# A MoE stage whose steps are ordered by a planner: talking-heads attention into a SoLU MoE on one core

## The chip, the core and the metric

One Trainium2 chip, one of its cores. The metric is the device time of one execution in microseconds. The core has five engines, each with its own queue that it works through strictly in order: PE (TensorE, matmuls), DVE (VectorE), ACT (ScalarE), POOL (GpSimd) and SP (SyncE, which issues DMAs). An instruction that waits holds everything behind it in its queue.

## The reference, cut to what matters

```python
# attention: batch 4, 12 heads, 448 tokens, head dimension 64
scores = einsum('bhij,hg->bgij', q @ k.T / 8, w_pre);  attn = softmax(scores)
x = (einsum('bhij,hg->bgij', attn, w_post) @ v)  ->  1792 tokens x 768
# MoE: d_model 768, d_ff 1024
h = x @ w_in;  solu = h * softmax(h)
ln = (solu - mean) / sqrt(var + 1e-6) * g_ln
out = ln @ w_out
```

[...] Each fp32 matmul of the MoE is three fp16 matmuls on operands split in a high and a low half (high by high, high by low, low by high).

## The kernel before, in words

**Attention** takes the first two thirds of the run. Its instructions are given as tasks to the class `Plan`: each task names its engine and a duration, the tasks it comes after, a due time, and the ring of buffers that it takes a slot of, with the tasks that free the slot. `Plan.order` simulates the engines: again and again it takes the engine and the task that can start earliest; among the tasks of an engine that can start within 0.143 us of the first one it prefers the one with the smallest due time. What comes out is one list, written into the queues in that order. The planner fixes only the order; semaphores still make each instruction wait for its data.

**The MoE** comes behind that list and is written out by hand. Its unit is a tile of 128 tokens, 14 of them; the three tiles of the last batch, whose x is still on the chip, come first, the other 11 are fetched back from DRAM (`x_fetch`, 6 pieces per batch). For tile t:
- `hidden(t)` (L876): 36 matmuls on PE into one of three PSUM bank pairs. Tile 0's are already in the attention's plan.
- `solu_head(t)`: DVE takes the maximum (L1387), ACT the exponential (L1390).
- `solu_mean(t)`: DVE guards and inverts the sum and multiplies (L1401); that product is the last reader of the bank pair. ACT squares (L1405), DVE forms the variance (L1408), POOL its power -1/2 (L1411).
- `ln(t)`: a Newton step on DVE (L1418 to L1426), POOL applies the norm (L1427), ACT makes the high half (L1430), POOL the low half (L1432).
- `turn(t)`: two transposing DMAs on SP (L1442), into a ring of 9.
- `project(t)`: 48 matmuls (L1458) by w_out into two banks, one for each half of the output columns, then a copy on ACT (L1466) and the store.

**w_out** is converted beside it, in 8 chunks of 128 rows. A chunk is fetched into one of two buffers (`cv`, L775), and goes through `convert_steps`: exponent (DVE, L790), rebias (ACT, L793), sign (DVE, L796), mantissa (DVE, L801), join (DVE, L806), product (POOL, L809); an absmax on ACT (L1351) ends it and frees the buffer. When all 8 are through, the joint maximum is taken on DVE, spread over the partitions by one matmul in PE's queue (L243), and turned into a scale; then each chunk is split into its two halves (high on ACT, L271; low on DVE, L276).

What sets the order is one loop over t. Iteration t issues the second half of tile t's softmax, `project(t - 11)`, `hidden(t + 1)`, the head of tile t + 1, `ln(t)`, the fetch of chunk t + 2 and `turn(t - 1)`. The steps of a chunk stand at lettered places inside (`work(t, "a")` to `"i"`), one chunk for each iteration: exponent and rebias of chunk t + 1 at place d of iteration t, the rest at a to e of the next. The 8 splits stand at places 9h to 10f, and `project(0)` in iteration 11.

Of the kernel before, what the change touches and what calls it, by code (L numbers as in the profile page):

```python
# [152 lines left out]
def kernel(  # L153
# [600 lines left out]

    def x_fetch(b, i, pool):
# [517 lines left out]
    with tc.manual_schedule():  # L1273
# [34 lines left out]
        nc.vector.tensor_tensor(out=ic, in0=i_post, in1=i_wi, op=ALU.mult)  # L1308
        nc.vector.tensor_scalar(out=ib, in0=i_v, scalar1=ic, scalar2=2.0**E_X, op0=ALU.mult, op1=ALU.mult)
        for b in range(B):  # L1310
            t0, t1 = -(-b * S // 128), (b + 1) * S // 128
            nc.vector.tensor_copy(out=ch[:, 0, t0:t1], in_=ib[:, b : b + 1].to_broadcast([128, t1 - t0]))
            n0 = (b + 1) * S - t1 * 128
            if n0:
                nc.vector.tensor_copy(out=ch[0:n0, 0, t1 : t1 + 1], in_=ib[0:n0, b : b + 1])
                nc.vector.tensor_copy(out=ch[n0:128, 0, t1 : t1 + 1], in_=ib[n0:128, b + 1 : b + 2])
        for i, m in ((1, -1.0), (3, 2.0**E_LN)):
            nc.vector.tensor_scalar(out=ch[:, i], in0=ch[:, 0], scalar1=m, scalar2=None, op0=ALU.mult)
        nc.vector.scalar_tensor_tensor(
            out=ch[:, 2], in0=ch[:, 0], scalar=1.0 / DFF, in1=ch[:, 0], op0=ALU.mult, op1=ALU.mult  # L1320
        )

# [20 lines left out]
        def convert_w_out(kc):  # L1343
            if kc % 4 == 0:
                wo_raw.append(raw_p.tile([128, KFF // 2, DM], F32, tag="raw", name=f"wo{kc}"))
            t = wo_raw[kc // 4][:, kc % 4]
            ex = parts64(f"wo{kc}")[2].bitcast(F32)
            exponent, rebias, sign, mantissa, join, product = convert_steps(t, f"wo{kc}")

            def absmax():  # L1350
                nc.scalar.activation(out=ex, in_=t, func=AF.Abs, accum_out=am_o[:, kc : kc + 1])  # L1351

            for i, place, f in zip(
                (kc - 1, kc - 1, kc, kc, kc, kc, kc),
                "ddabcce",
                (exponent, rebias, sign, mantissa, join, product, absmax),
            ):
                fill.setdefault((i, place), []).append(f)
# [14 lines left out]
        def split_w_out(kc):  # L1373
            x = wo_raw[kc // 4][:, kc % 4]
            split_hi(wo_h[:, kc], x, gs_wo[:, kc : kc + 1])
            split_lo(wo_l[:, kc], x, gs_wo[:, kc : kc + 1], wo_h[:, kc])

        lnp = {}

        heads, late = {}, []  # L1380

        def solu_head(t):

            ps = hps.pop(t).rearrange("p n f -> p (n f)")
# [8 lines left out]
        def solu_mean(t):
            ps, sm, u = heads.pop(t)
            v, y = (ms_p.tile([128, 1], F32, tag=n, name=f"{n}_{t}") for n in ("v", "y"))
            nc.vector.tensor_scalar(out=sm, in0=sm, scalar1=1e-9, scalar2=None, op0=ALU.add)
            work(t, "a")
            nc.vector.reciprocal(out=sm, in_=sm)
            work(t, "b")
            su, nmu, sq = (ms_p.tile([128, 1], F32, tag=n, name=f"{n}_{t}") for n in ("su", "nmu", "sq"))  # L1400
            nc.vector.scalar_tensor_tensor(  # L1401
                out=u, in0=ps, scalar=sm, in1=u, op0=ALU.mult, op1=ALU.mult, accum_out=su
            )
            nc.vector.tensor_scalar(out=nmu, in0=su, scalar1=-1.0 / DFF, scalar2=None, op0=ALU.mult)
            nc.scalar.activation(out=junk, in_=u, func=AF.Square, bias=nmu, accum_out=sq)  # L1405
            work(t, "c")
            work(t, "d")
            nc.vector.tensor_scalar(  # L1408
                out=v, in0=sq, scalar1=ch[:, 2, TURNS[t] : TURNS[t] + 1], scalar2=1e-6, op0=ALU.mult, op1=ALU.add
            )  # L1410
            nc.gpsimd.tensor_tensor(out=y, in0=v, in1=half_p, op=ALU.pow)  # L1411
            late.append((u, nmu, v, y))

        def ln(t):

            u, nmu, v, y = late.pop()
            z, rs, nm = (ms_p.tile([128, 1], F32, tag=n, name=f"{n}_{t}") for n in ("z", "rs", "nm"))
            nc.vector.scalar_tensor_tensor(out=z, in0=y, scalar=v, in1=y, op0=ALU.mult, op1=ALU.mult)  # L1418
            work(t, "e")
            nc.vector.tensor_scalar(out=z, in0=z, scalar1=-0.5, scalar2=1.5, op0=ALU.mult, op1=ALU.add)  # L1420
            work(t, "f")
            nc.vector.scalar_tensor_tensor(
                out=rs, in0=z, scalar=ch[:, 3, TURNS[t] : TURNS[t] + 1], in1=y, op0=ALU.mult, op1=ALU.mult
            )
            work(t, "g")
            nc.vector.tensor_scalar(out=nm, in0=nmu, scalar1=rs, scalar2=None, op0=ALU.mult)  # L1426
            nc.gpsimd.tensor_scalar(out=u, in0=u, scalar1=rs, scalar2=nm, op0=ALU.mult, op1=ALU.add)  # L1427
            lh = h_p.tile([128, DFF], F16, tag="lh", name=f"lh_{t}")
            ll = h_p.tile([128, DFF], F16, tag="ll", name=f"ll_{t}")
            nc.scalar.copy(out=lh, in_=u)  # L1430
            work(t, "h")
# [4 lines left out]
        lts = {}

        def turn(t):
            lt = lts[t] = []
            for x, z in zip(lnp.pop(t), "hl"):  # L1440
                y = lt_p.tile([128, KFF, 128], F16, tag=f"t{z}", name=f"lt{z}_{t}")
                nc.sync.dma_start_transpose(out=y, in_=x)  # L1442
                lt.append(y)

        def project(t):
            lt = lts.pop(t)
            o = h_p.tile([128, DM], F32, tag="o", name=f"o_{t}")
            ends = [0, DM // 2, DM] if t < NT - 1 else [0, 2 * DM // 3, DM]
            ys = []
            for n, (c0, c1) in enumerate(zip(ends, ends[1:])):  # L1450
                y = (ps_x, ps_y)[n % 2].tile([128, 512], F32, tag="x", name=f"y{n}_{t}")
                ys.append((y[:, 0 : c1 - c0], slice(c0, c1)))

            for group in [ys] if t == 0 else [[y] for y in ys]:
                for kc in range(KFF):
                    for a, (xx, ww) in enumerate(((lt[0], wo_h), (lt[0], wo_l), (lt[1], wo_h))):
                        for y, cut in group:
                            nc.tensor.matmul(  # L1458
                                y,
                                xx[:, kc],  # L1460
                                ww[:, kc, cut],
                                start=(kc == 0 and a == 0),
                                stop=(kc == KFF - 1 and a == 2),
                            )
# [84 lines left out]
```

## Time and profile before

| | |
|---|---|
| median of 3 runs | 720.27 us (719.42 to 721.44) |
| the profiled execution, its own time | 722.47 us |
| its span, first to last instruction | 720.8 us |
| PE busy | 651.8 us, 90% |
| DVE, ACT, POOL busy | 500.4 (69%), 455.2 (63%), 282.7 us (39%) |
| chain that ended last, by engine | PE 49%, DVE 26%, DMA 8%, ACT 6% |
| mean granted TensorE clock | 0.971 |

A row of instructions gives the line of the kernel, engine, operation, output and input tiles with their shape, and the count. "Idle before" is the time in which the engine stood still just ahead of it, with what released it. PE's durations overlap, since matmuls are pipelined: starts are to be compared with starts. The granted clock is 1.00 at 2.4 GHz and 0.50 at 1.2 GHz; what lies between is a mean over both.

### The profile page before, as it was taken

The page shows a single profiled execution, that of the slowest core. Times are in us where ns is not written, and L with a number is a line of the kernel's source. Part 1 is how long each engine was busy: PE and PEld are TensorE (multiplying, and loading weights), DVE is VectorE, ACT ScalarE, POOL GpSimd, SP SyncE. Part 2 cuts the span into 40 slices and gives each one's busy share as a digit, 9 for nine tenths or more (in the row PEclk, how much of TensorE's full clock was granted, in tenths as well). Part 3 has the DMA queues.
Part 4 walks back from the last instruction along what each step waited for, and adds up shares of the span by engine and source line. Part 5 has one row for each costly group of instructions (what it writes and reads, how often), then busy time and mean ns, then how long its engine had stood idle before and what let it go on. Part 6 is the DMA issues. An engine that isn't in the chain of part 4 may idle for free.

```text
span 720.8 us, 17481 instructions
## 1 busy us (share of the span) xinstructions
PE 651.8 (90%) x6514; PEld 430.3 (60%) x6514; DVE 500.4 (69%) x1331; ACT 455.2 (63%) x977; POOL 282.7 (39%) x447
## 2 busy tenths in 40 slices
PE   1787999999899999799899899899978959999997
PEld 1545767777567777677676677664433424566664
DVE  6977998789977799977899898646888654200000
ACT  1757887998779888788799887414455553321111
POOL 3704682247742257731244235305655523310000
PEclk9899999999999999999999999999999978999999
DMA  9137458456776566997339432057657402263112
GB/s 230 40 78 203 162 148 198 150 184 201 209 152 139 142 200 186 219 208 228 134 134 272 177 93 67 1 166 207 146 125 130 82 1 52 51 117 81 45 51 60
DMA packets 114028, 98.51 MB, mean 137 GB/s; under 512 B 69604, under 2 KB 104600, under 8 KB 113944
## 3 DMA queue, kind: packets, MB, share of 16 engines
q1 hardware_dynamic: 108120, 83.62, 44.0%
q0 software_dynamic: 4416, 12.40, 6.2%
q10 hardware_dynamic: 1408, 1.38, 0.7%
q8 instruction: 51, 0.84, 0.5%
q14 instruction: 33, 0.27, 0.1%
HBM read 33.24 MB, written 9.63 MB: 59 GB/s over the span
## 4 chain that ended last, share of the span: by engine, by line
PE 49%; DVE 26%; DMA 8%; ACT 6%; issue 5%; POOL 4%; SPq 2%; POOLq 0%; DVEq 0%; ACTq 0%
PE y L1458 15%; PE po L659 14%; PE px L708 6%; PE pm L604 5%; PE ps L534 5%; DVE dead L614 5%; DVE s L551 4%; DMA cv_wo<-in_moe_w_out_dram 4%; PE ps_h L876 3%; DMA sr<-s 2%; ACT e L630 2%; DVE hl_k L276 2%; DVE sm L641 2%; DVE hl_q L276 1%; DVE u L1387 1%
## 5 line engine op out<-in xcount | busy, mean ns | idle before, releaser
L659 PE MATMUL po<-wr,e 128*112 128x120 f32 x1440 | 184.6, 279 | 15.3 <-POOL wr L651 12.3
L659 PEld LDWEIGHTS po<-wr,e 128*112 128x112 f32 x1440 | 161.4, 181 | 54.4 <-POOL wr L651 28.4
L651 POOL TENSOR_SCALAR wr<-wq,sm 128x120 f32<-128x120 f32 x180 | 70.8, 403 | 217.4 <-DVE sm L645 124.7
L630 ACT ACTIVATE e<-pm,nb,c_exp 128x448 f32<-128x448 f32 x180 | 131.9, 734 | 23.7 <-DVE dead L614 21.2
L614 DVE TENSOR_SCALAR_CACHE_REDUCE dead<-pm,c_nexp 128x448 f16<-128x448 f32 x180 | 121.6, 675 | 14.6 <-PE pm L604 8.4
L280 ACT COPY p_t<-po 112x480 f32<-112x480 f32 x180 | 109.7, 620 | 28.7 <-PE po L659 27.2
L551 DVE SCALAR_TENSOR_TENSOR s<-ps,s 120x448 f16<-120x448 f32 (+1 forms) x192 | 112.4, 616 | 19.0 <-ACT s L546 17.5
L546 ACT ACTIVATE s<-ps 120x448 f16<-120x448 f32 (+1 forms) x192 | 93.9, 546 | 23.7 <-PE ps L534 20.4
L876 PE MATMUL ps_h<-wi,xf 128*128 128x512 f16 x396 | 91.2, 392 | 6.5 <-DVE u L1401 6.5
L708 PE MATMUL px<-p_t,raw_v 112*64 112x120 f32 (+3 forms) x1632 | 88.2, 259 | 1.9 <-ACT e L630 0.8
L708 PEld LDWEIGHTS px<-p_t,raw_v 112*64 112x64 f32 x1632 | 76.0, 137 | 15.5 <-issue 9.3
L534 PE MATMUL ps<-k,q 64*64 64x448 f16 (+2 forms) x1008 | 79.5, 356 | 5.1 <-DVE s L551 3.3
L1458 PE MATMUL y<-wo_h,lth 128*128 128x384 f16 (+2 forms) x224 | 73.4, 334 | 7.2 <-ACT wo_h L271 7.2
L1458 PE MATMUL y<-wo_l,lth 128*128 128x384 f16 (+2 forms) x224 | 73.4, 334 | 2.2 <-DVE wo_l L276 2.0
L876 PEld LDWEIGHTS <-xf 128*128 128x128 f16 x396 | 40.0, 101 | 56.9 <-issue 13.8
L1458 PE MATMUL y<-wo_h,ltl 128*128 128x384 f16 (+2 forms) x224 | 73.2, 333 | 0.0
L1458 PEld LDWEIGHTS <-lth 128*128 128x128 f16 x448 | 44.6, 99 | 41.6 <-issue 13.5
L604 PE MATMUL pm<-sr,wp_hi 64*64 64x448 f16 x720 | 58.3, 362 | 5.6 <-DMA sr<-s 3.5
L1466 ACT ACTIVATE o<-y,c_out 128x384 f32<-128x384 f32 (+2 forms) x28 | 16.1, 578 | 70.7 <-PE y L1458 70.7
L534 PEld LDWEIGHTS <-q 64*64 64x64 f16 (+2 forms) x1008 | 31.9, 106 | 31.6 <-issue 15.3
L1432 POOL TENSOR_TENSOR ll<-u,lh 128x1024 f16<-128x1024 f32 x14 | 30.4, 2171 | 19.2 <-ACT lh L1430 19.2
L630 ACT ACTIVATION_READ_ACCUMULATOR e<-pm,nb,c_exp 128x1 f32 x180 | 37.7, 209 | 0.0
(180 smaller groups left out, 816.0 us busy)
## 6 DMA issues: line engine op xcount, KB each, us to landing
sr<-s SPq DMA_DIRECT2D x176, 210.0 KB
cv_wi<-in_moe_w_in_dram SPq DMA_DIRECT2D x24, 256.0 KB
cv_wo<-in_moe_w_out_dram SPq DMA_DIRECT2D x8, 768.0 KB
raw_k<-in_k_dram POOLq DMA_DIRECT2D x18, 224.0 KB, 4.0
raw_q<-in_q_dram POOLq DMA_DIRECT2D x18, 224.0 KB, 6.5
raw_v<-in_v_dram POOLq DMA_DIRECT2D x18, 224.0 KB, 5.4
xh<-xsh SPq DMA_DIRECT2D x9, 224.0 KB
xl<-xsl SPq DMA_DIRECT2D x9, 224.0 KB
```

The lines of the kernel that those rows point to most:

```text
L280: nc.scalar.copy(out=out, in_=in_)
L534: nc.tensor.matmul(sps[b, c, h + e][lo:hi], q2[b, g][rows, 2 * j + x, i0 + lo : i0 + hi], k1[b, g][rows, 2 * j + y], start=(a == 0), stop= ...
L546: nc.scalar.activation(out=s_t[b, c][0 : y.shape[0], h, 0], in_=y, func=AF.Copy, scale=2.0**-E_S)
L551: nc.vector.scalar_tensor_tensor(out=t[:, h, 1], in0=y, scalar=2.0**-E_S, in1=t[:, h, 0], op0=ALU.mult, op1=ALU.subtract)
L604: nc.tensor.matmul(pmx[b, u + i][64 * e : 64 * e + 64, 0:S], w[rows], sr[b, u][rows, e, z], start=(a == 0), stop=(a == 2),)
L614: nc.vector.tensor_scalar(out=dead, in0=pmx[b, u][:, 0:S], scalar1=c_nexp[0:UK, b : b + 1], scalar2=None, op0=ALU.mult, op1=ALU.min, accum ...
L630: nc.scalar.activation(out=ee[b, u], in_=pmx.pop((b, u))[:, 0:S], func=AF.Exp, bias=nbs.pop((b, u)), scale=c_exp[0:UK, b : b + 1], accum_o ...
L651: ENG[eng].tensor_scalar(out=w, in0=wq[0:UK, 0 : H * UN], scalar1=sm, scalar2=1.0, op0=ALU.mult, op1=ALU.mult)
L659: nc.tensor.matmul(ps[:, c * 120 : (c + 1) * 120], e[:, c * CP : (c + 1) * CP], w, start=True, stop=True)
L708: nc.tensor.matmul(xps[b, blk, g][e * 64 : e * 64 + 64, i, cut], raws["v", b, p][:, e, c * D : (c + 1) * D], next(x for y, x in block_view ...
L876: nc.tensor.matmul(ps[:, n], xx[:, kc, o : o + 128], ww[:, kc, n * 512 : (n + 1) * 512], start=(kc == 0 and a == 0), stop=(kc == KDM - 1 a ...
L1458: nc.tensor.matmul(y, xx[:, kc], ww[:, kc, cut], start=(kc == 0 and a == 0), stop=(kc == KFF - 1 and a == 2),)
```

## The change

The MoE's loop, its lettered places and the list of places for the splits go. Each step becomes a task of a second `Plan`, with an engine, a duration, a due time and its ring; the plan's order is written behind the attention's. The functions issue the same instructions as before, cut into single steps. The factors (`factors`, the small DVE operations ahead of the MoE), the load of g_ln and the fetches of x are tasks as well. `project` of tile 0 is cut into 16 tasks, one for each chunk of w_out and half of the output.

The due times: tile t at 7.75 t, chunk kc at 9.0 kc (its fetch 12 ahead, its absmax 8 behind), the joint maximum at 70, its spread at 70.5, the scale at 72, the splits at 73 + kc and 74 + kc, output tile t at 7.75 (t + 11).

```diff
-        SPL = "9h 9i 10a 10b 10c 10d 10e 10f".split()
...
-        for t in range(NT + LAG):
-            if t + 1 < KFF:
-                convert_w_out(t + 1)
-            if t < NT:
-                solu_mean(t)
-            if 0 <= t - LAG < NT:
-                project(t - LAG)
-            if t + 1 < NT:
-                hidden(t + 1)
-                work(t, "turn")
-                solu_head(t + 1)
-            if t < NT:
-                ln(t)
...
+        LAG = 11
+        moe = Plan(h=3, u=3, lh=2, ll=2, th=9, tl=9, cv=2, X=1, Y=1, o=2)
+        add = moe.add
...
+        for kc in range(KFF):
+            due = 9.0 * kc
+            add(("zF", kc), one(fetch_w_out, kc), {"sp": 0.65}, ..., due=due - 12,
+                ring="cv", until=[("zM", kc)], dma=(16, 786, 18.5))
+            prev = [("zF", kc)]
+            on = ({"dve": 0.8}, {"act": 0.9}, {"dve": 1.25}, {"dve": 0.65}, {"dve": 1.35}, {"pool": 1.85})
+            for i in range(6):
+                add(("zC", kc, i), one(w_out_step, kc, i), on[i], after=prev, ..., due=due + 1.2 * i)
+                prev = [("zC", kc, i)]
+            add(("zM", kc), one(w_out_max, kc), {"act": (1.0, 1.1)}, after=prev, due=due + 8)
+        add(("zx", 0), max_w_out, {"dve": (0.2, 0.35)}, after=[("zM", kc) ...] + [("zg",)], due=70.0)
+        add(("zx", 1), lambda e: o_steps[1][1](), {"pe": 0.25}, after=[("zx", 0)], due=70.5, ring="X", ...)
+        add(("zx", 2), lambda e: o_steps[2][1](), {"dve": (0.2, 0.3)}, after=[("zx", 1)], due=71.0)
+        add(("zx", 3), scale_w_out, {"dve": 1.1}, after=[("zx", 2)], due=72.0)
+        for kc in range(KFF):
+            add(("zH", kc), one(w_out_hi, kc), {"act": 0.83}, after=[("zx", 3)], due=73.0 + kc)
+            add(("zL", kc), one(w_out_lo, kc), {"dve": 1.0}, after=[("zH", kc)], due=74.0 + kc)
...
+        for t in range(NT):
+            T = 7.75 * t
+            add(("zh", t), one(hidden, t) if t else (lambda e: None), {"pe": 7.75} if t else ...,
+                after=[("zX", x, i) ...], due=T - 7.75, ring="h", until=[("zp", t)])
+            chain = [
+                ("zn", solu_max, {"dve": (1.25, 1.34)}, 0.0, "u", ("zo", t)),
+                ("ze", solu_exp, {"act": (1.2, 1.3)}, 1.3, None, None),
+                ("za", solu_guard, {"dve": (0.08, 0.17)}, 2.6, None, None),
+                ("zb", solu_invert, {"dve": (0.08, 0.17)}, 2.7, None, None),
+                ("zp", solu_product, {"dve": (1.25, 1.34)}, 2.8, None, None),
...
+                ("zu", ln_apply, {"pool": (1.15, 1.25)}, 7.0, None, None),
+                ("zl", ln_hi, {"act": (0.95, 1.05)}, 8.3, "lh", ("zT", t, "h")),
+                ("zo", ln_lo, {"pool": (2.1, 2.15)}, 9.4, "ll", ("zT", t, "l")),
+            ]
...
+            T = 7.75 * (t + LAG)
+            for n in range(2):
+                parts = [[kc] for kc in range(KFF)] if t == 0 else [list(range(KFF))]
+                for j, kcs in enumerate(parts):
+                    add(("zP", t, n, kcs[-1]), one(project, t, n, kcs), {"pe": ...},
+                        after=[("zT", t, "h"), ("zT", t, "l")] + [("zL", kc) for kc in kcs],
+                        due=T + (3.9 * n if t else 0.9 * j + 0.45 * n), ring=None if j else "XY"[n], ...)
...
+        for _, e, _, run in moe.order():
+            run(e)
```

## Rows read from the trace of the kernel before

**Rows 1.** Costliest groups of the page: busy us, mean ns, idle before, its releaser.

```profile
L876 PE MATMUL ps_h<-wi,xf 128*128 128x512 f16 x396 | 91.2, 392 | 6.5 <-DVE u L1401 6.5
...
L1458 PE MATMUL y<-wo_h,lth 128*128 128x384 f16 (+2 forms) x224 | 73.4, 334 | 7.2 <-ACT wo_h L271 7.2
L1458 PE MATMUL y<-wo_l,lth 128*128 128x384 f16 (+2 forms) x224 | 73.4, 334 | 2.2 <-DVE wo_l L276 2.0
```

**Rows 2.** PE in order of time: start us, us, instruction, count, idle before.

```profile
495.17 31.24 PE L876 MATMUL ps_h<-wi,xf 128*128 128x512 f16 x144
528.20 7.93 PE L876 MATMUL ps_h<-wi,xf 128*128 128x512 f16 x36 [1.79 <-DVE u L1401]
538.26 9.62 PE L876 MATMUL ps_h<-wi,xf 128*128 128x512 f16 x36 [2.13 <-DVE u L1401]
...
580.09 0.80 PE L1458 MATMUL y<-wo_h,lth 128*128 128x384 f16 x2 [4.09 <-ACT wo_h L271]
...
598.40 8.97 PE L876 MATMUL ps_h<-wi,xf 128*128 128x512 f16 x36
```

**Rows 3.** Busy us by stretch; the last three: PEclk, DMA share, GB/s.

```profile
480.00:496.00 16.00, 16.00 (x76) 7.21 (x74) 13.09 (x27) 8.55 (x12) 5.93 (x4) 1.00 1.00 287
...
560.00:600.00 40.00, 30.58 (x121) 13.63 (x119) 25.13 (x66) 21.31 (x30) 16.02 (x13) 0.80 0.19 37
```

**Rows 4.** The chain of waits in order of time: start us, us, what.

```profile
505.38 4.64 DMA cv_wo<-in_moe_w_out_dram
...
520.67 1.35 DVE cv_wo L790
...
522.15 1.21 DVE u L1387 x2
...
525.53 5.07 DMA cv_wo<-in_moe_w_out_dram
...
535.59 5.09 DMA cv_wo<-in_moe_w_out_dram
...
615.17 7.77 PE ps_h L876 x36
622.94 93.61 PE y L1458 x576
```

**Rows 5.** DVE in order of time, columns as in rows 2.

```profile
501.32 0.56 DVE L790 TENSOR_SCALAR cv_wo<-cv_wo 128x768 uint32<-128x768 uint32 x1 [4.08 <-DMA cv_wo<-in_moe_w_out_dram]
...
524.71 0.15 DVE L1396 TENSOR_SCALAR sm<-sm 128x1 f32<-128x1 f32 x1 [0.54 <-ACT u L1390]
...
530.69 1.40 DVE L790 TENSOR_SCALAR cv_wo<-cv_wo 128x768 uint32<-128x768 uint32 x1 [0.94 <-DMA cv_wo<-in_moe_w_out_dram]
```

**Rows 6.** Operations on w_out's buffers: ns min/median/max, first and last start.

```profile
L790 DVE TENSOR_SCALAR cv_wo<-cv_wo x8: 556/1370/1847, 480.5 to 550.5; 128x768 uint32<-128x768 uint32 x8
L793 ACT ACTIVATE cv_wo<-cv_wo,bias x8: 934/935/937, 481.1 to 552.3; 128x768 uint32<-128x768 uint32 x8
L796 DVE SCALAR_TENSOR_TENSOR cv_wo<-cv_wo x8: 948/1568/1571, 483.7 to 555.0; 128x768 uint32<-128x768 uint32 x8
L801 DVE TENSOR_SCALAR cv_wo<-cv_wo x8: 560/562/1460, 484.6 to 556.6; 128x768 uint32<-128x768 uint32 x8
L806 DVE SCALAR_TENSOR_TENSOR cv_wo<-cv_wo x8: 951/1498/2382, 486.5 to 558.4; 128x768 f32<-128x768 uint32 x8
L809 POOL TENSOR_TENSOR wo<-cv_wo x8: 1847/1848/1872, 487.8 to 560.0; 128x768 f32<-128x768 f32 x8
L1351 ACT ACTIVATE cv_wo<-wo x8: 830/832/836, 490.6 to 562.5; 128x768 f32<-128x768 f32 x8
```

**Rows 7.** POOL in order of time, columns as in rows 2.

```profile
522.23 0.55 POOL L1411 TENSOR_TENSOR y<-v,half_p 128x1 f32<-128x1 f32 x1 [0.62 <-DVE v L1408]
524.35 1.20 POOL L1427 TENSOR_SCALAR u<-u,rs,nm 128x1024 f32<-128x1024 f32 x1 [1.57 <-DVE nm L1426]
526.71 2.22 POOL L1432 TENSOR_TENSOR ll<-u,lh 128x1024 f16<-128x1024 f32 x1 [1.16 <-ACT lh L1430]
```

More of the change, by code (lines that the diff above doesn't have):

```diff
@@ L1340, in fetch_w_out, with w_out_step @@
         def fetch_w_out(kc):
             fetch64(w_out[kc * 128 : (kc + 1) * 128], cv_p, "cv", DM, f"wo{kc}")
[L1343 to L1346, printed above, removed]
-            ex = parts64(f"wo{kc}")[2].bitcast(F32)
[L1348 to L1358, printed above, removed]
+        def w_out_step(kc, i):
+            if i == 0:
+                if kc % 4 == 0:
+                    wo_raw.append(raw_p.tile([128, KFF // 2, DM], F32, tag="raw", name=f"wo{kc}"))
+                wo_steps[kc] = convert_steps(wo_raw[kc // 4][:, kc % 4], f"wo{kc}")
+            wo_steps[kc][i]()
@@ L1393, in solu_mean, with w_out_hi @@
[L1393 to L1400, printed above, removed]
-            nc.vector.scalar_tensor_tensor(
-                out=u, in0=ps, scalar=sm, in1=u, op0=ALU.mult, op1=ALU.mult, accum_out=su
-            )
[L1404 to L1407, printed above, removed]
+        def w_out_hi(kc):
+            split_hi(wo_h[:, kc], wo_raw[kc // 4][:, kc % 4], gs_wo[:, kc : kc + 1])
@@ L1436 @@
[L1436 to L1464, printed above, removed]
-                for y, cut in group:
-                    nc.scalar.activation(out=o[:, cut], in_=y, func=AF.Copy, scale=c_out)
-                    if t == NT - 1:
-                        store(t, o, cut)
-            if t < NT - 1:
-                store(t, o, slice(0, DM))
@@ L1473, in store, with emit, stores @@
+        def emit(t, n):
+            if n == 0:
+                outs[t] = h_p.tile([128, DM], F32, tag="o", name=f"o_{t}")
+            c = slice(*ENDS[t][n : n + 2])
+            nc.scalar.activation(out=outs[t][:, c], in_=ys.pop((t, n)), func=AF.Copy, scale=c_out)
+        def stores(t, cut):
             done, runs = 0, []
@@ L1487 @@
-        fill[KFF + 1, "e"] = [scale_w_out]
-        for kc, w in enumerate(SPL):
-            fill.setdefault((int(w[:-1]), w[-1]), []).append(lambda kc=kc: split_w_out(kc))
-        LAG, TURN = 11, 1
-        fetch_w_out(0)
-        fetch_w_out(1)
-        nc.sync.dma_start(out=g_sb, in_=g_ln.rearrange("(k p) -> p k", p=128))
+            return sorted(runs, key=lambda r: -r[0])
+        one = lambda f, *a: lambda e: f(*a)
+        add(("zf",), factors, {"dve": 2.2}, due=0.0)
+        add(("zg",), lambda e: nc.sync.dma_start(out=g_sb, in_=g_ln.rearrange("(k p) -> p k", p=128)), {"sp": 0.6}, due=3.0, dma=(8, 4, 1))
@@ new lines @@
+        add(("zx", 0), max_w_out, {"dve": (0.2, 0.35)}, after=[("zM", kc) for kc in range(KFF)] + [("zg",)], due=70.0)
+        add(
+            ("zx", 1),
+            lambda e: o_steps[1][1](),
+            {"pe": 0.25},
+            after=[("zx", 0)],
+            due=70.5,
+            ring="X",
+            until=[("zx", 2)],
+        )
+        add(("zx", 2), lambda e: o_steps[2][1](), {"dve": (0.2, 0.3)}, after=[("zx", 1)], due=71.0)
+        add(("zx", 3), scale_w_out, {"dve": 1.1}, after=[("zx", 2)], due=72.0)
```

284 lines of the change are left out of this document (212 added, 72 removed).

## Prediction

> **What bounds the kernel now.** I read first the costliest groups of the page, with the idle time ahead of them, then PE's timeline over the MoE, then the chain of waits in that stretch, and last the operations of w_out's conversion and the queues of DVE and POOL.
>
> The groups [rows 1] show where PE waits in the MoE: 6.5 us ahead of the hidden matmuls, for DVE's product (L1401), which frees a PSUM bank; and 7.2 + 2.2 us ahead of the output matmuls, for the two splits of w_out. Together 15.9 us. The timeline [rows 2] shows the places: ahead of tiles 7 to 10, and around output tile 0 (580 to 598). The granted clock is 0.80 from 560 to 600, a mix of its two levels, and 1.00 where PE is never idle [rows 3]. So the waits are paid twice: hidden tile 8, after a 2.13 us wait, takes 9.62 us where tile 7 took 7.93 [rows 2], and tile 10 repeats it to the digit. From 615 to the end PE's work is the whole chain, 7.77 us for a hidden tile, 93.61 us for the last 12 output tiles, 7.80 each [rows 4].
>
> What the order by hand costs beyond PE's own work:
> - idle 15.9;
> - three hidden tiles at a lower clock, 2 x (9.62 - 7.93) + (8.97 - 7.93) = 4.4;
> - output tile 0: from 580.09 to 598.40 are 18.31 us, of which 5.3 are idle already counted (9.4 less the 4.09 ahead of it) and 7.80 is the tile's work [rows 2, 4]; 5.2 are left.
>
> Sum 25.5 us. PE's work stays what it is, so this is the most that another order can give.
>
> Why PE waits: the chain [rows 4] repeats every 10.0 us (520.67 to 530.7): w_out's chunk lands 5.1 us after its fetch leaves, DVE does its exponent, only then the tile's next steps, and an absmax on ACT ends the round and frees a buffer for the next fetch. Call L the time from a chunk's landing to the end of its absmax: the chunk whose exponent starts at 520.67 frees the fetch that leaves at 535.59, so L is 15 us. With two buffers that is (5.1 + 15) / 2 = 10.05 us per chunk, and by hand one tile goes with each chunk. PE needs 7.77 for a tile, and falls back by 2.3 each time once its three banks are full.
>
> **The change part by part.**
>
> *No instruction goes or comes*; all are put in another order on the five queues. The fixed round of one chunk and one tile is gone: a chunk is due every 9.0 us, a tile every 7.75, each step separately. PE's 25.5 us come back in so far as the others can keep to 7.77 per tile. I cost each that could be late next.
>
> *DVE's work.* In a round of 10.02 us DVE waits 0.94 for the chunk and 0.54 for exp [rows 5], and the four conversion steps take 1.37 + 1.57 + 0.56 + 1.50 = 5.0 by their medians [rows 6]; 3.5 is the tile's share. The shortest of the four sum to 3.0, so 2.0 is delay. POOL explains it: the sign step of this round follows the guard of 524.71 [rows 5], so with its 1.57 us it ran to about 526.35, while POOL applied the norm from 524.35 to 525.55 [rows 7], and ended 0.8 us after it, near its undisturbed 0.95; join, undisturbed 0.95 as well, has a median of 1.50 and follows POOL's subtraction, 526.71 to 528.93, in the same way [rows 6, 7]. POOL is busy 0.55 + 1.20 + 2.22 + 1.85 = 5.8 of 10.05 us, 58% [rows 6, 7]; with a tile per 7.77 and a chunk per 9 it would be 3.97 / 7.77 + 1.85 / 9 = 72%. Bounds for a chunk on DVE: 3.0 (never delayed) and 7.3 (the four maxima). I take 3.0 + 2.0 x 72 / 58 = 5.5. The planner's own figures are 4.05, so its order will run late on DVE.
>
> The Trainium skill, "SBUF — State Buffer", section "Who interferes with whom", bears on this: it says that DVE and GpSimd share a pair of SBUF ports under an exclusive lock, so that the second to come waits for the first to end. The ends just read agree. By that rule a denser order delays DVE more, which speaks against this change: a chunk of 5.5, and PE's wait below. By the planner's fixed 4.05 the ledger below would be 8.7 us shorter and the sum 694.8, with no wait at all.
>
> *The ledger up to w_out's scale.* In the order by hand DVE sat 4.08 us for chunk 2, until 501.32 [rows 5]; before it the input fetches fill the DMA engines (share 1.00 from 480 to 496 [rows 3]), and the planner issues them early too, so I leave that landing. Tile 2's hidden matmuls end at 495.17 [rows 2], so its 3.5 us fit into the gap. By the due times DVE then has, before the joint maximum of w_out (due 70): chunks 2 to 7, tiles 3 to 8 and tile 9's maximum, 1.2 [rows 4]: 6 x 5.5 + 6 x 3.5 + 1.2 = 55.2, so 556.5. It waits too: 1.48 per round now, of which the planner should fill most by putting other steps there; I leave 30% of six rounds, 2.7. So the maximum comes at 559.2. It is followed on PE by the spreading matmul, due 70.5, between tile 10 (due 69.75) and tile 11 (77.5). PE without waits ends tile 10 at 495.17 + 8 x 7.77 = 557.3. **PE waits 1.9 us there, and I add one slow tile, 1.7: cost 3.6.** Tiles 8 to 10 need DVE's product three tiles back; by the same count it is 2 to 3 us ahead of them each time, so nothing there, but the margin is thin.
>
> *The fetches.* They still wait for the buffer. Chunk 3 lands at the latest where it lands now (505.38 + 4.64 = 510.0 [rows 4]), then the odd chunks go round twice more: absmax of chunk 7 ends at 510 + 2 x 5.1 + 3 L. The seven steps undisturbed sum to 0.56 + 0.94 + 0.95 + 0.56 + 0.95 + 1.85 + 0.83 = 6.6 [rows 6]; by hand L is 15.0. The due times spread a chunk over 9 us; with 2 us of delays I take L = 11: 553, under the ledger's 559. With L = 13 the two are equal.
>
> *w_out's split and output tile 0.* Scale (a few one-column steps), one split step on ACT (absmax has its width: 0.83) and one on DVE (1.5) are some 3 us behind the spread, an estimate, while hidden tile 11 runs for 7.77. Tile 0 of the output (due 85.25, as hidden tile 12) comes with or after tile 12, each chunk of it on its own; the eight split steps on DVE have join's shape, so I take its 0.95 to 1.50 [rows 6], among the steps of tiles 9 and 10, done near 577. PE reaches its last chunk at 557.3 + 3.6 + 2 x 7.77 + 7 = 583. No cost, cover 6 us.
>
> *SP's queue.* Transposes and fetches stand in one queue as before; a transpose that waits for POOL holds the fetch behind it. The planner counts that in its own times; if it happens it lengthens L.
>
> *The last twelve output tiles* were already PE alone and stay so; the end (last copy and store) is unchanged.
>
> Sum against the profiled execution: 722.47 (span 720.8) - 25.5 + 3.6 = 700.6. It is 2.2 above the median of the timed runs, 720.27; on that median: **698.4**.
>
> **The rivals.**
>
> *A. DVE, or the conversion, sets the pace.* For: the planner takes 4.05 for chunks of 5 us, and margins are 2 to 3 us. If L stays 15, the maximum is at 510 + 10.2 + 45 = 565.2, 7.9 us behind PE; if a chunk costs DVE 6.5, the ledger gives 565.2 as well. With one or two slow tiles (1.7 to 3.4) 9.6 to 11.3 are lost: 704.4 to 706. At the four maxima (7.3 a chunk, +10.8 on the ledger) the wait is 12.7 and, over three or four tiles, 5 to 7 more: 712 to 714. Against: once DVE is the late one, its own waits vanish.
>
> *B. It doesn't do what it says.* The planner writes nearly the same round, a tile's step behind each chunk's step, and the period stays 10: 720. Against: two due times of different period.
>
> *C. Slower.* Queues are in order, and the spread stands in PE's between two hidden tiles, all later tiles behind it. If the conversion gets longer than now, PE stands at this one place. It must come 25.5 - 1.7 = 23.8 us late to lose everything, at 581.1: L = (581.1 - 520.2) / 3 = 20.3. From there the change is slower, 3 us for each us of L; at L = 22, 725. For it: seven steps over three engines, each able to queue behind a tile's step that itself waits, and SP holding the fetch. Against: by hand, with one step per place, L is 15.
>
> **How the numbers follow.** Forecast (PE nearly gap-free, 695 to 703): 0.58. A up to 712: 0.22; A beyond 712 but still faster: 0.06. B: 0.06. C: 0.08. A measurement can't tell less than 0.3%, 2.2 us, from no change. Faster: 0.58 + 0.22 + 0.06 = 0.86; same: 0.06; slower: 0.08. Range: the floor 720.27 - 25.5 = 694.8, less 0.8 for scatter, up to 712, which leaves out some 0.2 above it. The forecast's own range is 694 to 703.
>
> **What would show it.** Right: hidden tiles 3 to 13 of PE at 7.8 us each without gaps over 2 us; granted clock 1.00 from 496 on but for one stretch; w_out's first split before 566 (now the output matmuls wait for it until 580.09 [rows 2]); the first output matmul between 569 and 577; the output tiles ending near 694. DVE busy over 90% from 500 to 556. The chunks' steps no longer next to the same step of a tile. Wrong: fetches still 10 us apart (B), PE idle ahead of the spread or of output tile 0 for more than 5 us (A), for more than 24 (C), or sign and join above 2 us each on DVE.

## The result and the profile after

697.82 us (median of 4 runs, 694.18 to 699.51) against 720.21: ratio 0.9681, interval 0.964 to 0.9722. Forecast were 698.4, with 694 to 712. The profiled execution took 698.26 us, 24.2 less than the one before, with a span of 696.5.

The costliest groups of the page that answer to [rows 1] (behind the bar: busy us, mean ns, idle before, its releaser):

```profile
L880 PE MATMUL ps_h<-wi,xf 128*128 128x512 f16 x396 | 86.0, 379 | 1.5 <-DVE u L1412 1.5
...
L1485 PE MATMUL y<-wo_h,lth 128*128 128x384 f16 (+2 forms) x224 | 73.0, 326 | 0.0
L1485 PE MATMUL y<-wo_l,lth 128*128 128x384 f16 (+2 forms) x224 | 73.0, 326 | 0.0
```

Of the 15.9 us in which PE waited, 1.5 are left, all ahead of hidden matmuls; the output matmuls never wait. PE in order of time, columns as in [rows 2]:

```profile
495.61 70.09 PE L880 MATMUL ps_h<-wi,xf 128*128 128x512 f16 x324
565.54 0.38 PE L243 MATMUL spread_wo<-ident,amx_wo 128*128 128x128 f32 x2
567.42 7.93 PE L880 MATMUL ps_h<-wi,xf 128*128 128x512 f16 x36 [1.50 <-DVE u L1412]
575.19 0.33 PE L1485 MATMUL y<-wo_h,lth 128*128 128x384 f16 x1
...
582.99 7.93 PE L880 MATMUL ps_h<-wi,xf 128*128 128x512 f16 x36
```

Nine hidden tiles (324 matmuls, tiles 3 to 11) run without a gap in 69.9 us, then the spread, the one wait, tile 12, output tile 0, tile 13. Tile 12 takes 7.93 us, so the wait was not paid a second time in clock. The granted clock (third column from the end) is 1.00 in all three stretches, against 0.80 from 560 to 600 in [rows 3]:

```profile
496.00:528.00 32.00, 32.00 (x150) 14.48 (x149) 26.74 (x55) 16.57 (x26) 20.34 (x15) 1.00 0.70 148
528.00:560.00 32.00, 32.00 (x150) 14.55 (x149) 29.69 (x58) 17.77 (x27) 23.46 (x15) 1.00 0.51 123
560.00:600.00 40.00, 38.50 (x206) 20.07 (x205) 32.98 (x79) 25.29 (x38) 22.16 (x15) 1.00 0.25 51
```

The third number of a line, behind PE's and the weight loads', is DVE: 29.7 of 32 us busy from 528 to 560 (49.4 of 56 from 500 to 556). The chain of waits, as in [rows 4], is PE's own work but for one stretch between 534 and 567, in which it runs over DVE, with single steps on POOL and ACT (three of PE's pieces, its last one among them):

```profile
476.24 58.40 PE ps_h L880 x270
...
575.35 7.80 PE y L1485 x48
...
590.92 101.41 PE y L1485 x624
```

The MoE starts 0.44 us later than before (PE's tile 3 at 495.61 against 495.17) and its last output matmul ends at 692.33 against 716.55: the MoE is 24.7 us shorter (from tile 3's start to the end of the last output matmul, called its length below: 221.4 before, 196.7 after). The start moves from run to run: in three profiles of the changed kernel tile 3 begins at 491.5 to 497.4, and the length is 196.7 in each. That start is where these three differ. Of the kernel before, and of each kernel tried below, there is one profile.

### The profile page after: what moved, and what is told of

Same layout as the page of the kernel before. It is cut to its first block, busy times and chain, and to the rows that moved or that the text cites. A ratio compares the mean times of both kernels' runs of the same rounds, so it can differ in the third digit from the quotient of the medians.

```text
span 696.5 us, 17486 instructions
## 1 busy us (share of the span) xinstructions
PE 641.7 (92%) x6514; PEld 427.5 (61%) x6514; DVE 505.9 (73%) x1332; ACT 453.3 (65%) x977; POOL 291.9 (42%) x447
## 3 DMA queue, kind: packets, MB, share of 16 engines
q10 hardware_dynamic: 1408, 1.38, 0.8%
## 4 chain that ended last, share of the span: by engine, by line
PE 59%; DVE 25%; ACT 4%; issue 4%; DMA 3%; POOL 3%; SPq 0%; POOLq 0%; DVEq 0%; ACTq 0%
PE y L1485 16%; PE po L659 15%; PE ps_h L880 11%; PE px L708 7%; PE pm L604 5%; PE ps L534 5%; DVE dead L614 5%; DVE s L551 5%; ACT e L630 2%; DMA sr<-s 2%; DVE hl_k L276 2%; DVE sm L641 2%; DVE hl_q L276 1%; POOL wr L651 1%; DMA rep<-in_w_post_dram 1%
## 5 line engine op out<-in xcount | busy, mean ns | idle before, releaser
L546 ACT ACTIVATE s<-ps 120x448 f16<-120x448 f32 (+1 forms) x192 | 93.9, 545 | 25.5 <-PE ps L534 21.7
L880 PE MATMUL ps_h<-wi,xf 128*128 128x512 f16 x396 | 86.0, 379 | 1.5 <-DVE u L1412 1.5
L534 PEld LDWEIGHTS <-q 64*64 64x64 f16 (+2 forms) x1008 | 32.3, 107 | 32.1 <-issue 15.9
```

The source lines that it names most:

```text
L534: nc.tensor.matmul(sps[b, c, h + e][lo:hi], q2[b, g][rows, 2 * j + x, i0 + lo : i0 + hi], k1[b, g][rows, 2 * j + y], start=(a == 0), stop= ...
L546: nc.scalar.activation(out=s_t[b, c][0 : y.shape[0], h, 0], in_=y, func=AF.Copy, scale=2.0**-E_S)
L880: nc.tensor.matmul(ps[:, n], xx[:, kc, o : o + 128], ww[:, kc, n * 512 : (n + 1) * 512], start=(kc == 0 and a == 0), stop=(kc == KDM - 1 a ...
```

## The experiments

Two questions stayed open. What does the gain come from: the place of output tile 0 and the splits, or the tie of one tile to one chunk in each iteration? And why is the conversion (w_out's 64-bit floats into 32-bit ones) no faster, as the fetches show? SP in order of time:

```profile
505.21 1.22 SPq L779 DMA_DIRECT2D cv_wo<-in_moe_w_out_dram  x1
...
515.46 0.35 SPq L779 DMA_DIRECT2D cv_wo<-in_moe_w_out_dram  x1
...
546.19 0.33 SPq L779 DMA_DIRECT2D cv_wo<-in_moe_w_out_dram  x1
```

A fetch leaves every 10.1 to 10.6 us (the last three rounds, 30.73 us, 10.24 each), much as before. Theory 1 at the start: two separate losses, the tie (10.9 us, at the hidden tiles) and output tile 0's place (14.6 us).

**e1: by hand, the hidden tile first**

```diff
-            if 0 <= t - LAG < NT:
-                project(t - LAG)
             if t + 1 < NT:
                 hidden(t + 1)
                 work(t, "turn")
                 solu_head(t + 1)
+            if 0 <= t - LAG < NT:
+                project(t - LAG)
```

Expected:

> The order by hand, with one edit: in each iteration hidden(t + 1) and the head of tile t + 1 stand ahead of project(t - 11). Theory 1 (two separate losses: the hidden tiles wait since each tile step stands behind a chunk that has to land, 10.9 us; and output tile 0 stands in PE's queue ahead of a hidden tile that could run, 14.6 us): hidden tile 12 runs from about 576 while the splits are made, output tile 0 ends near 597 instead of 598.4 with tile 12 then already done, so 9 to 10 us come back: about 710.5; the waits ahead of tiles 7 to 10 stay 6.5 us. Rival (everything hangs on the late conversion, the place of output tile 0 is nothing by itself): PE only waits later, under 3 us come back, 717 to 720.

713.5 us against 720.87, ratio 0.9898 (0.9865 to 0.993): 7.4 us. By the MoE's length, 211.1 us, it is 10.3.

```profile
538.99 9.62 PE L876 MATMUL ps_h<-wi,xf 128*128 128x512 f16 x36 [2.13 <-DVE u L1401]
...
568.79 15.70 PE L876 MATMUL ps_h<-wi,xf 128*128 128x512 f16 x72
...
589.45 0.48 PE L1458 MATMUL y<-wo_h,lth 128*128 128x384 f16 x2 [1.06 <-ACT wo_h L271]
...
594.91 0.48 PE L1458 MATMUL y<-wo_h,lth 128*128 128x384 f16 x2 [2.62 <-ACT wo_h L271]
...
597.60 7.93 PE L876 MATMUL ps_h<-wi,xf 128*128 128x512 f16 x36
```

Tiles 11 and 12 now run in one piece (72 matmuls) while the splits are made, and the wait of 4.09 us ahead of output tile 0 and the tile of 8.97 us behind it [rows 2] are gone. Four waits inside output tile 0 stay, 4.8 us with the two not shown. The tiles 7 to 10 wait as before, and two of them still take 9.62 us. Output tile 0's place is a loss of its own. Its size is 7.4 us by the times and 10.3 by the one profile; the 9 to 10 expected lie between.

**e2: the planner's order, tied**

```diff
-                add((n, t), ..., behind=[(n, t - 1)] if t else [], ...)
+                add((n, t), ..., behind=([(n, t - 1)] if t else [])
+                    + ([("zC", t + 1, 0)] if n == "zv" and t + 1 < KFF else []), ...)
-            add(("zM", kc), one(w_out_max, kc), ..., after=prev, due=due + 8)
+            add(("zM", kc), one(w_out_max, kc), ..., after=prev, behind=[("ze", kc + 1)], due=due + 8)
```

Expected:

> The planner's order, with the tie of the order by hand put back: the variance of tile t stands on DVE behind the exponent of chunk t + 1, and the absmax of chunk t on ACT behind the exponential of tile t + 1; all else is still the planner's. Theory 1: tiles go at the chunks' period of 10 us again, PE waits about 6 to 8 us ahead of hidden tiles 7 to 12 with two or three tiles at a lower clock, output tile 0 keeps its good place: 705 to 710. Rival (the gain is all from where the splits and output tile 0 stand): within 1.5 us of the changed kernel, 697 to 699.

696.75 us, ratio 0.9656 (0.9622 to 0.9689): as the changed kernel. One tile again goes with each chunk (on DVE each exponent stands directly ahead of a variance), but a round takes 8.9 us (the last 9.2) and not 10.05, by the fetches:

```profile
515.01 0.35 SPq L779 DMA_DIRECT2D cv_wo<-in_moe_w_out_dram  x1
...
523.94 0.33 SPq L779 DMA_DIRECT2D cv_wo<-in_moe_w_out_dram  x1
```

PE falls back 1.2 us per round instead of 2.3, and no hidden tile waits. So one tile per chunk isn't what costs by itself, and theory 1's part on the tie falls. The edit didn't put the whole order by hand back, though. The planner runs tiles one further ahead of the chunks: by hand the maximum of tile 4 follows chunk 4's exponent, here that of tile 5 does. So the absmax of chunk 3 stands on ACT behind the exponential of tile 4, which was long done, and ahead of tile 5's:

```profile
516.02 1.19 ACT L1395 ACTIVATE u<-ps_h,nb,ch 128x1024 f32<-128x1024 f32 x1
...
522.98 0.84 ACT L1354 ACTIVATE cv_wo<-wo 128x768 f32<-128x768 f32 x1 [0.22 <-POOL wo L813]
...
523.82 1.19 ACT L1395 ACTIVATE u<-ps_h,nb,ch 128x1024 f32<-128x1024 f32 x1
```

The changed kernel runs its tiles one ahead as well. The rival's number came out, and its reason isn't shown by it.

**e3: a third buffer**

```diff
-        cv_p = ctx.enter_context(tc.tile_pool(name="cv", bufs=2))
+        cv_p = ctx.enter_context(tc.tile_pool(name="cv", bufs=3))
-        lt_p = ctx.enter_context(tc.tile_pool(name="lt", bufs=9))
+        lt_p = ctx.enter_context(tc.tile_pool(name="lt", bufs=8))
-        junk = wt_p.tile([128, DFF], F32, name="junk")
+        junk = wt_p.tile([128, DFF], F16, name="junk")
-        moe = Plan(..., th=9, tl=9, cv=2, ...)
+        moe = Plan(..., th=8, tl=8, cv=3, ...)
```

Expected:

> The planner's order with a third buffer for w_out's chunks (to make room the transposed rings have 8 instead of 9, and the scratch of the square is fp16). Theory 1a (DVE has no more left for the conversion: it is over 90% busy from 500 to 560, tiles go first by PE's pace and chunks get the rest): fetches leave earlier, but the last absmax comes no more than 2 us earlier than 561.5, L grows from 15 to 20 and more; time within 1.5 us of the changed kernel. Rival 1b (the round of two buffers, 5.1 + 15 us for two chunks, sets the conversion): the last absmax comes 8 to 15 us earlier, PE's 1.5 us wait goes, 696.

698.91 us, ratio 0.9687 (0.9654 to 0.972): as the changed kernel. The last fetch leaves at 526.9, 19 us earlier than the 546.19 above, and yet the last absmax begins only 2.8 us earlier than the changed kernel's 560.7 (last number ahead of the shape). Of both, 2.7 us is this profile's earlier start (tile 3 at 492.95 instead of 495.61); counted from there, the fetch is 16.6 us earlier and the absmax 0.1:

```profile
L1354 ACT ACTIVATE cv_wo<-wo x8: 827/837/846, 487.9 to 557.9; 128x768 f32<-128x768 f32 x8
```

The landed chunks lie and wait: under the planner the buffers' round doesn't set the conversion's pace. That it is what DVE has left fits, with DVE busy 56.6 of the 60 us from 500 to 560 here and 52.9 in the changed kernel; whether DVE's work or the place that the planner gives the steps in its queue sets it wasn't separated.

**e4: one buffer**

```diff
-        cv_p = ctx.enter_context(tc.tile_pool(name="cv", bufs=2))
+        cv_p = ctx.enter_context(tc.tile_pool(name="cv", bufs=1))
-        moe = Plan(..., cv=2, ...)
+        moe = Plan(..., cv=1, ...)
```

Expected:

> The planner's order with one buffer for w_out's chunks instead of two: each fetch waits for the absmax of the chunk before it. It tests the prediction's slower case, a conversion that comes late. By it, with L of 10 to 12 for a chunk that meets no other: 15 to 17 us per chunk, last absmax at 600 to 615, PE through with all hidden tiles at 582 and idle until 604 to 619, 22 to 37 us less at most the 1.5 it waits now, some slow clock: 718 to 735. Rival (the planner gets by with less, L near the undisturbed 6.6): 12 us per chunk, last absmax near 578, 698 to 702.

721.16 us, ratio 1.0005 (0.9986 to 1.0023): the whole gain is lost. PE:

```profile
496.04 85.63 PE L880 MATMUL ps_h<-wi,xf 128*128 128x512 f16 x396
598.78 0.79 PE L243 MATMUL spread_wo<-ident,amx_wo 128*128 128x128 f32 x2 [17.11 <-DVE amx_wo L264]
602.28 0.48 PE L1485 MATMUL y<-wo_h,lth 128*128 128x384 f16 x1 [2.71 <-ACT wo_h L271]
```

Fetches leave 15.4 to 15.7 us apart, the last absmax ends at 598.2, and PE, through with all 14 hidden tiles, waits 17.1 + 2.7 us. So the prediction's slower case is real, but its point lies elsewhere: the planner saw the late conversion and put the spread behind tile 13 instead of between two tiles, so the last absmax may end near 598, not 581, before the change is a loss.

**Theory 2.** By hand, absmax of chunk t stands on ACT behind the exponential of tile t + 1, that behind its maximum on DVE, and that behind the exponent of chunk t + 1, which waits for its landing. So a buffer comes free only when the other one's chunk has landed, and the two never carry two fetches at once: fetch, exponent, variance, maximum, exponential, absmax, fetch is one loop of 5.1 + 1.4 + 0.1 + 1.2 + 1.3 + 0.8 = 9.9 us. The chain before the change shows it closed; these pieces stand between those of [rows 4]:

```profile
522.03 0.12 DVE v L1408
...
524.49 0.19 ACT u L1390
524.68 0.83 ACT cv_wo L1351 x2
```

In e2 the loop is open, since its absmax doesn't wait for the exponential of the tile behind the landing.

**e5: by hand, the exponent behind the head of the next tile**

```diff
-                "ddabcce",
+                "eeabcce",
```

Expected:

> The order by hand, with one edit: exponent and rebias of chunk t + 1 stand at place e of iteration t, behind the head of tile t + 1, instead of at d ahead of it. Theory 2 (by hand the two buffers never carry two fetches at once: fetch, exponent, maximum, exponential, absmax and the next fetch form one loop of 10.05 us, since the absmax that frees a buffer stands behind an exponential that stands behind the landing of the other buffer's chunk): the loop is cut, a round takes DVE's own 8.5 to 9.0 us, fetches leave every 8.5 to 9 us, absmax of the last chunk ends near 555 instead of 563.5, the waits ahead of hidden tiles 7 to 10 shrink from 6.5 to under 2 us, and since output tile 0 keeps its bad place, about 8 us come back: 711 to 713. Rival (the tie of one tile to one chunk costs by itself, whatever the loop): rounds stay near 10, 718 to 721.

716.18 us, ratio 0.993 (0.9906 to 0.9955): 5.1 us by the ratio, 5.8 between the medians, 6.1 by the MoE's length (215.3). Fetches at 519.10 and 528.41, 9.3 apart; the last absmax ends at 556.2, and the hidden tiles wait 3.2 us in all (0.43 of it ahead of the tile before these, not shown), and each then takes 7.93 us. PE in order of time:

```profile
541.91 7.93 PE L876 MATMUL ps_h<-wi,xf 128*128 128x512 f16 x36 [1.38 <-DVE u L1401]
551.23 7.93 PE L876 MATMUL ps_h<-wi,xf 128*128 128x512 f16 x36 [1.38 <-DVE u L1401]
...
572.89 0.80 PE L1458 MATMUL y<-wo_h,lth 128*128 128x384 f16 x2 [5.75 <-ACT wo_h L271]
```

The exponent also takes 0.56 us here instead of 1.37 (medians), which alone could shorten the loop to about 9.2. But the chain of waits has no landing in it any more: from one rebias (L793) to the next it runs over a chunk's and a tile's steps on DVE, POOL and ACT, 9.3 us each time:

```profile
528.38 0.83 ACT cv_wo L793
...
534.24 1.85 POOL wo L809
...
537.68 0.83 ACT cv_wo L793
```

So the loop is cut, with a round of 9.3 instead of the 8.5 to 9.0 that I expected. Of the earlier conversion PE gets little, since it then waits for the splits at output tile 0 for 12.0 us instead of 9.4.

**e6: both edits**

Both diffs above together. Expected:

> The order by hand with both edits: exponent and rebias at place e, and hidden(t + 1) with the head ahead of project(t - 11). Theory 2: the two losses are separate and both edits add up, 7.3 (measured for the second alone) + 8: 704 to 706; what then stays over the changed kernel (some 7 us) is the splits, still spread over two iterations. Rival (they share one cause, the late conversion): no more than 2 us better than the better of the two alone, 710 to 712.

706.35 us, ratio 0.9783 (0.9746 to 0.9819): 15.6 us. Alone the two gave 7.4 and 5.1, each known to some 2 us either way; by the MoE's length they gave 10.3 and 6.1, and both give 14.1 (207.3). So whether the gains add up exactly isn't shown. Either way both together give at least 3.8 us more than the better one alone, where the rival had 2 at most. So the losses don't share one cause.

**e7: the norm on ACT**

```diff
-            nc.gpsimd.tensor_scalar(
-                out=u, in0=u, scalar1=sc[t, "rs"], scalar2=sc[t, "nm"], op0=ALU.mult, op1=ALU.add
-            )
+            nc.scalar.activation(out=u, in_=u, func=AF.Identity, scale=sc[t, "rs"], bias=sc[t, "nm"])
...
-                ("zu", ln_apply, {"pool": (1.15, 1.25)}, 7.0, None, None),
+                ("zu", ln_apply, {"act": (1.05, 1.15)}, 7.0, None, None),
```

Expected:

> The planner's order, with the norm of each tile applied on ACT (Identity with scale and bias) instead of POOL; the planner has its duration. POOL loses 1.2 to 1.8 of some 6 us per round, ACT gains 1.15. If DVE's delays behind POOL cost PE its last wait: the first Newton step on DVE falls from a mean of 0.58 us to under 0.4, a chunk's four steps from 4.4 to 3.9 or less, the 1.5 us wait ahead of hidden tile 12 goes, PE has no gap over 0.5 us: 1 to 1.5 us less than the changed kernel, 696. Rival (ACT in its place becomes late: exponentials queue behind the norm): a wait of 2 us or more at the hidden tiles, 699 to 703.

700.04 us, ratio 0.9696 (0.967 to 0.9723), against 0.9645 (0.9615 to 0.9676) for the changed kernel measured beside it (e8): not better. A chunk's four steps fall to 3.97 us, the mantissa's never wait, and the wait ahead of tile 12 goes; the first Newton step falls to a mean of 0.51 us only. But the last absmax ends 4.8 us later, counted from the first fetch, and PE waits for the joint maximum:

```profile
567.44 0.49 PE L243 MATMUL spread_wo<-ident,amx_wo 128*128 128x128 f32 x2 [2.46 <-DVE amx_wo L264]
```

Two delays lead there. POOL's product for the last absmax ends at 561.78, but on ACT the norm (562.59) and the high half (563.86) of a tile come first, and the absmax starts at 564.81. And the first step of the joint maximum (128 x 8) takes 1.22 us instead of 0.20, from 565.97 to 567.19, while POOL's subtraction ends at 567.16. So the wait has moved. This run doesn't clear DVE's delays behind POOL: 1.0 of its 2.46 us is one. That the norm on ACT makes the absmax late fits, and wasn't tried by itself.

**e8 and e11: the changed kernel again.** Expected:

> The changed kernel again, as the comparison on the same chip: 697 to 698.5, and PE's waits over the MoE again 1.5 us at one place, if the single profile of it was typical.

> The changed kernel once more, for e10 on the same chip: 696.5 to 698, PE's one wait 1.5 us.

696.57 (ratio 0.9645, 0.9615 to 0.9676) and 698.16 us (0.9676, 0.9652 to 0.9701), in both the same 1.50 us ahead of tile 12 and no other wait.

**e9: by hand, the splits in one row as well**

```diff
-        SPL = "9h 9i 10a 10b 10c 10d 10e 10f".split()
+        SPL = "9g 9g 9g 9g 9h 9h 9h 9h".split()
```

Expected:

> The order by hand with three edits: the two of e6 and all 8 splits of w_out at places g and h of iteration 9, right behind the scale, instead of spread over 9h to 10f. If what e6 still lacks is the splits' place: PE's waits inside output tile 0 (4.9 us and slow clock around them) go, the splits come in one row of 8 to 10 us from about 571, tile 0 runs without a gap behind hidden tile 12, 5 to 7 us better than e6: 699.5 to 701.5, within 4 us of the changed kernel; what is left is the rounds of 9.3 us (3 us of waits at the hidden tiles). Rival (the tile chain of 10 and 11, now behind the splits on ACT and DVE, comes late instead and PE waits ahead of hidden tile 13 or a later output tile): 704 to 707.

705.61 us, ratio 0.9774 (0.9749 to 0.98): by the times no different from e6, by the MoE's length (205.0) 2.3 us better. The waits inside output tile 0 shrink to 0.3 us. Ahead of the hidden tiles 8 to 10 stand 1.13, 1.37 and 1.38 us, the last two as in e6, and 0.64 ahead of tile 13. The longest is new:

```profile
597.08 0.48 PE L1458 MATMUL y<-wo_h,lth 128*128 128x384 f16 x1 [2.85 <-ACT o L1466]
```

These 2.85 us stand ahead of output tile 1, which waits for ACT to copy tile 0 out, and ACT for an exponential that came late. My expectation was wrong and the rival's came out. PE's 7.6 us of waits here, 6.1 more than in the changed kernel, are about the 7 us between the two.

**e10: measured durations for the planner**

```diff
-            on = ({"dve": 0.8}, {"act": 0.9}, {"dve": 1.25}, {"dve": 0.65}, {"dve": 1.35}, {"pool": 1.85})
+            on = ({"dve": 0.98}, {"act": 0.92}, {"dve": 0.95}, {"dve": 1.0}, {"dve": 1.45}, {"pool": 1.93})
...
-                ("zu", ln_apply, {"pool": (1.15, 1.25)}, 7.0, None, None),
+                ("zu", ln_apply, {"pool": (1.55, 1.63)}, 7.0, None, None),
...
```

Expected:

> The changed kernel with the durations given to the planner replaced by the means of its trace (exponent 0.98, sign 0.95, mantissa 1.0, join 1.45, product 1.93, norm 1.6, first Newton step 0.5 us and so on); no instruction differs, only their order. The planner then puts the spread behind hidden tile 12 and output tile 0 behind tile 13. Expected: PE's 1.5 us ahead of hidden tile 12 go and none comes in its place, the last output matmul 1 to 1.5 us earlier: 0.1 to 0.2% better than the changed kernel in the same call, hardly to be told by the times. Rival (the rings, not the durations, made product 9 late; or output tile 0 so late that the transposed ring of 9 holds tiles 9 to 13 back): a wait of 1.5 us or more, same or slower.

699.5 us, ratio 0.969 (0.9665 to 0.9714), against 0.9676 for the changed kernel measured beside it (e11): the same. The wait at tile 12 goes as expected. That none would come in its place was wrong: 2.2 us come ahead of output tile 1, again for ACT's copy:

```profile
496.30 77.86 PE L880 MATMUL ps_h<-wi,xf 128*128 128x512 f16 x360
...
592.18 0.32 PE L1485 MATMUL y<-wo_h,lth 128*128 128x384 f16 x1 [2.22 <-ACT o L1497]
```

No version was measurably better than the changed kernel. The MoE of e2's one profile is 0.7 us shorter (196.0 against 196.7), which its times can't tell.

## Why the prediction was right, point by point

**The time: right, and its closeness partly luck.** Forecast was a gain of 25.5 - 3.6 = 21.9 us. The medians fell by 22.4, the MoE of the two profiles by 24.7; the interval of the ratio, 20.0 to 25.9 us, holds all three. So the 0.6 us between 698.4 and 697.82 says little.

**The ceiling of 25.5 us: nearly right.** The MoE became 24.7 us shorter with 1.5 left, together 26.2. The sum missed some 0.16 us for each of the five waits behind a hidden tile: it counts a wait from the tile's end, 7.93 us after its start, and without a wait the next one starts 7.77 after it. The end behind the last matmul is unchanged, as forecast.

**PE's wait: smaller than forecast, its place and its reason wrong.** I had 1.9 us at the spread and 1.7 for a slow tile; measured are 1.5 ahead of hidden tile 12 and no slow tile. I had looked at DVE's product, which frees the bank, for tiles 8 to 10 only, with a thin margin. Tile 12 waits for that of tile 9 (L1412, from 566.08). Tile 9's matmuls are done near 550, and the buffer for its result is free from 554.2, when POOL's last step of tile 6 ends; but its maximum (L1384) starts at 562.95, behind chunk 7's last steps and tile 8's Newton step. DVE, in order of time, then ACT:

```profile
558.89 1.80 DVE L1444 SCALAR_TENSOR_TENSOR z<-y,v 128x1 f32<-128x1 f32 x1 [0.45 <-POOL y L1439]
...
560.92 1.86 DVE L1450 SCALAR_TENSOR_TENSOR rs<-z,ch,y 128x1 f32<-128x1 f32 x1
...
562.95 1.28 DVE L1384 TENSOR_SCALAR_CACHE_REDUCE u<-ps_h,ch 128x1024 f32<-128x1024 f32 x1
...
564.38 0.16 DVE L264 TENSOR_REDUCE amx_wo<-am_o 128x1 f32<-128x8 f32 x1
564.49 1.28 DVE L1384 TENSOR_SCALAR_CACHE_REDUCE u<-ps_h,ch 128x1024 f32<-128x1024 f32 x1
...
566.08 1.28 DVE L1412 SCALAR_TENSOR_TENSOR u<-ps_h,sm,u 128x1024 f32<-128x1024 f32 x1
```

```profile
564.32 1.21 ACT L1395 ACTIVATE u<-ps_h,nb,ch 128x1024 f32<-128x1024 f32 x1 [2.68 <-DVE u L1384]
```

The lines at 558.89 and 560.92 are one-column parts of that Newton step and took 0.22 us each where nothing held them (below). Together they are 3.2 us too long, more than the 1.5 that PE waits; the other two profiles of this kernel show the same two. That PE wouldn't wait without them is worked out from these rows, not tried. The maximum of tile 10 (564.49) stands ahead of the product too, but cost it at most 0.1 us: tile 9's exponential on ACT ends as late.

**The ledger: errors that cost nothing.** The joint maximum (its second step is the line at 564.38) came at 564.1, not 559.2. A chunk took 0.98 + 0.95 + 1.01 + 1.45 = 4.4 us on DVE by its means, less than my 5.5, but the tiles took more. Tile 2's maximum and product (500.30 and 503.34) don't fit into the gap but stand ahead of chunk 2's exponent (504.55). A tile's share is 3.8 us in the round of [rows 5], not 3.5: I took off durations, which overlap at their ends, instead of distances from start to start. And there are the 3.2 us above. From 501.32 to 564.14 the conversion's steps take 26.2 us (33.0 forecast), the tiles 30.8 (22.2), DVE's waits 5.6 (2.7). It was harmless since the planner put the spread behind tile 11, not tile 10; PE got there at 565.5.

**The fetches: wrong.** I took L = 11, and it stayed at 15 for the chunks that free a buffer for another; only the last two, which free none, took some 12 and 10 us, by a transfer of 5.1. That was my sign for "the period stays 10", the case of no gain, and the sign was wrong too: chunks at 10 us cost nothing when tiles don't queue behind their landing. With the fetches about as far apart, the product of tile 4 starts at 521.85 in the changed kernel and at 526.86 by hand. e3 shows that the buffers' round doesn't set L here; by hand it was the loop (e5). I had read the loop's length in the chain [rows 4], but taken its two buffers for two fetches in flight. (5.1 + 15) / 2 and the loop's sum both give 10, and only the second explains why moving one step shortens it.

**Delays behind POOL: they moved.** My 72 / 58 was wrong for the chunk. The four steps of [rows 6] after the change (ns min/median/max):

```profile
L794 DVE TENSOR_SCALAR cv_wo<-cv_wo x8: 545/686/1934, 481.5 to 551.1; 128x768 uint32<-128x768 uint32 x8
...
L800 DVE SCALAR_TENSOR_TENSOR cv_wo<-cv_wo x8: 945/949/959, 484.6 to 554.3; 128x768 uint32<-128x768 uint32 x8
L805 DVE TENSOR_SCALAR cv_wo<-cv_wo x8: 550/568/2369, 485.6 to 556.0; 128x768 uint32<-128x768 uint32 x8
L810 DVE SCALAR_TENSOR_TENSOR cv_wo<-cv_wo x8: 949/1401/2235, 486.2 to 556.6; 128x768 f32<-128x768 uint32 x8
```

The sign step, 1.57 us in the median before, is never delayed now. Two one-column steps of the tile are now and then, whose means were 0.21 and 0.22 before (here from 477 to 586):

```profile
L1444 DVE SCALAR_TENSOR_TENSOR z<-y,v 128x1 f32<-128x1 f32 x11 | 6.3, 575 | 3.0 <-POOL y L1439 3.0
L1450 DVE SCALAR_TENSOR_TENSOR rs<-z,ch,y 128x1 f32<-128x1 f32 x11 | 4.1, 369 | 0.4
```

In the DVE rows above, the first of them takes from 558.89 to 560.69 and the second from 560.92 to 562.78; POOL's product and subtraction end at the same moments, 560.68 and 562.77:

```profile
558.83 1.85 POOL L813 TENSOR_TENSOR wo<-cv_wo 128x768 f32<-128x768 f32 x1
560.64 2.13 POOL L1470 TENSOR_TENSOR ll<-u,lh 128x1024 f16<-128x1024 f32 x1
```

A chunk and a tile together have 4.4 + 0.5 us of steps and delays of this kind against 4.8 before. What a step lost depended on where the order put it, not on POOL's share as I scaled it. The Trainium skill ("SBUF — State Buffer", "Who interferes with whom") describes a lock between DVE and GpSimd that the second to come waits out; these ends agree with it.

**Output tile 0: right.** It ran from 575.19 to 582.99 without a gap, within my 569 to 577 for its start, with w_out's splits ready ahead of each chunk. Two of my signs for "right" failed all the same: the first split began at 571.06, not before 566, and DVE was busy 88% from 500 to 556, not over 90.

**The gain's source.** By hand, e1, e5 and e6 give back 15.6 us in two places, the order of one hidden tile and output tile 0, and the loop of the fetch. The other 7 us by the times, 8 to 11 by the MoE's length, lie mainly in the waits that e6 and e9 keep: rounds of 9.3 us against PE's 7.77, and ACT or the splits late around output tiles 0 and 1. Which of the planner's placements removes these wasn't separated.

## What to carry to other kernels

With in-order queues, ask of each buffer what the instruction that frees it stands behind: if that is the landing of the other buffer, two buffers work as one, and the period is one transfer plus the steps between. The ceiling of a reordering is the bound engine's idle time plus what its lower clock costs after it; near that ceiling other engines' steps need not get faster, only stop standing ahead of what the bound engine needs. A planner's list goes by its own durations: read from the trace which instruction stands ahead of the one that was waited for, not from due times. And compare two profiles from a common event: the MoE of the changed kernel started up to 5.9 us apart in its three and was equally long to 0.01 us.

## What was not expected of the hardware

One-column steps of DVE (128 x 1) took up to 1.92 us instead of 0.22 while POOL worked on tensors of 768 or 1024 columns, ending with POOL's instruction to 0.02 us. A wait of 1.5 us on PE left the granted clock at 1.00 in three profiles of three. Waits of 2.13 us were followed by a tile of 9.62 us instead of 7.93 (twice before the change [rows 2], twice in e1), but waits of 2.46 us (e7) and 2.22 us (e10) left it at 1.00. So here the length of the last wait alone doesn't tell whether the clock falls.
